# Three pieces of the second expert matrix in column halves in place of five, and twelve output rows stored in halves in place of eighteen

## The chip, the cores and the metric

One core of a Trainium2 chip runs the whole kernel. The metric is device time in microseconds (us) of one execution, as the median of several runs. A profile of one execution gives the times of every instruction and DMA packet.

## The reference

The computation is an attention stage with learned pooling, followed by a soft mixture of experts:

```python
a = softmax(phi, axis=2)                       # q, k, v: (8, 8, 576, 64); phi: (8, 8, 576, 32)
k_m, v_m = einsum(a, k), einsum(a, v)
x = softmax(q @ k_m.T / 8) @ v_m               # reshaped to x: (4608, 512)
logits = x @ moe_phi                           # (4608, 32): 8 experts with 4 slots each
d = softmax(logits, axis=0)
slot_input = d.T @ x                           # (32, 512)
slot_out[e] = relu(slot_input[e] @ w1[e]) @ w2[e]   # w1: 8 x 512 x 1024, w2: 8 x 1024 x 512
out = softmax(logits, axis=1) @ slot_out       # (4608, 512), float32
```

The change lies in the last two lines: how the second expert matrices `w2` are loaded, and in which order the output is made and stored.

## The kernel before

The kernel writes its work as a list of operations into a `Plan`. The planner gives each a time by its own cost table and sends them to the engines in that order; every engine then works through its own list in order. All transfers, loads and stores, are issued by SyncE (SP) on one queue, in the planner's order. A transfer may only be issued once the eighth transfer before it has landed, because eight semaphores take turns.

The second expert layer (`expert_out`, `mult`) reads `w2` in 16 pieces of 1 MB, two per expert. The first experts' pieces come early. The later ones come as whole matrices of 2 MB (one transfer), one single piece of 1 MB, and, for the last `NT` pieces, in column halves: `tail_out` first loads the left 256 columns of all `NT` pieces, and then the right 256 columns of all of them. A half of a piece is two transfers of 256 KB (128 partitions, two runs of 1 KB each). `tail_mult(d, n)` multiplies half `d` (0 is left, 1 is right) of tail piece `n`. The left products accumulate in the bank `kvbank`, the right products in `scbank`.

When the left products are done, `slot_sums(0)` copies the bank (L1349), sums it with a matmul (L1357) and splits the result into two parts in `sr` (L1364, L1369). From then on the left 256 columns of output rows can be made. When the right products are done, `slot_sums(1)` does the same for the right columns.

The output has 4 blocks of 128 partitions (`bp` 0 to 3) with 9 rows per partition in each (`j` 0 to 8), 36 "rows" of 128 x 512 in all, 256 KB each. A row is made on TensorE by `out_mult` (L1603: two matmuls of 256 columns for a half row, of 512 for a whole one), copied from the bank to the arena by VectorE (L1580) or ScalarE (L1579), and stored (L1616). The first two rows are made straight from the sums (`direct`, L1587).

The first `NA` groups of three rows are made in halves: their left halves while the right columns of `w2` still arrive, their right halves after the right sum. A half group is stored by one transfer of 384 KB in runs of 1 KB, except that the three rows of group 0 are stored singly (128 KB each). All later rows are made and stored whole. `RIGHT[m]` says behind which left half group the right product of tail piece `m` stands on TensorE (-1: ahead of all of them); the right sum follows the last of these.

Of the kernel before, what the change touches and what calls it, by code (L numbers as in the profile page):

```python
# [20 lines left out]
class Plan:  # L21
# [24 lines left out]
    def add(self, eng, cost, fn, r=(), w=(), also=(), pri=None, dma=0.0, slack=0.0, after=()):  # L46
        cost, ni = cost if isinstance(cost, tuple) else (cost, 4)
        i = len(self.ops)
        deps = set()
        tiles = {}  # L50
        for x in r:
            for key in x:
                tiles[key[0]] = None
                if key in self.last_w:
                    deps.add(self.last_w[key])
        for x in w:
            for key in x:
                tiles[key[0]] = None
                if key in self.last_w:
                    deps.add(self.last_w[key])  # L60
                deps.update(self.reads.get(key, ()))
        for x in w:
            for key in x:
                self.last_w[key] = i
                self.reads[key] = []
        for x in r:
            for key in x:
                self.reads.setdefault(key, []).append(i)
        deps.discard(i)
        deps.update(after)  # L70
        tiles = [t for t in tiles if t.pool is not None]
        for t in tiles:
            t.users += 1
        need = tiles + [t for t in also if t not in tiles]
        if pri is None:
            pri = self.phase[0]
            self.phase[0] += self.phase[1]
        self.ops.append((eng, cost, fn, deps, pri, dma, tiles, need, slack, ni))
        return i
# [191 lines left out]
def kernel(  # L271
# [27 lines left out]
    E, DM, FF = w1.shape  # L299
# [56 lines left out]
    def shaped(off, shape):  # L356
        n = 1
        for x in shape:
            n *= x
        a = arena[:, off: off + n]  # L360
        if len(shape) > 1:
            names = "abcd"[: len(shape)]
            a = a.rearrange(
                f"p ({' '.join(names)}) -> p {' '.join(names)}",
                **dict(zip(names[:-1], shape[:-1])),
            )
        return a, (off, n)

    def area(off, shape, n, below=(), fifo=False):

        size = shaped(off, shape)[1][1]
        xs = [shaped(off + i * size, shape) for i in range(n)]
        return Slots([a for a, _ in xs], [r for _, r in xs], below, fifo)
# [917 lines left out]
    w2s = area(W0, [2 * W_SZ], NW // 2, [ws, *early])  # L1291
    ots = area(W0, [OT_SZ], NOUT, [w2s])
    b0 = W0 + NOUT * OT_SZ
    big = {6: area(b0, [6 * DM], 1, [w2s]), 9: area(b0 + 6 * DM, [9 * DM], 1, [w2s])}
    wqs = Slots(
        [qtile[:, i * W_SZ: i * W_SZ + W_SZ] for i in range(2)],
        [(TOP + i * W_SZ, W_SZ) for i in range(2)], [qs],
# [25 lines left out]


    EG = 4
    NT, NA = 5, 6
    ONES = 2
    RIGHT = (-1, 1, 1, 2, 2)
    SLOT_AT = (20.06, 20.08, 20.1)
    hTb = hTs.tile().split(E // EG)  # L1330
    hT = lambda: hTb.ap.rearrange("p (x y) -> p x y", x=8)
# [13 lines left out]
    def slot_sums(d, middle=lambda: None):  # L1345
        x = slice(d * HD, d * HD + HD)
        add(
            *((ACT, act(HD)) if d else (DVE, dve(HD))),
            lambda: (nc.scalar.copy if d else nc.vector.tensor_copy)(  # L1349
                accs.ap[:, x], pacc[d].ap[:, 0, :HD]  # L1350
            ),
            r=[pacc[d]], w=[accs.part(d)],
        )
        y = middle()
        z = add(
            PE, 0.5,
            lambda: nc.tensor.matmul(  # L1357
                so[d].ap[:, :HD], rep.rearrange("p a n -> p (a n)"), accs.ap[:, x],
                start=True, stop=True,
            ),  # L1360
            r=[accs.part(d), rep_b], w=[so[d]], after=[y] if y is not None else (),
        )
        add(
            ACT, act(HD), lambda: nc.scalar.copy(sr.ap[:, 0, x], so[d].ap[:, :HD]),  # L1364
            r=[so[d]], w=[sr.part(d)],
        )
        add(
            DVE, dve(HD),
            lambda: nc.vector.tensor_tensor(  # L1369
                sr.ap[:, 1, x], so[d].ap[:, :HD], sr.ap[:, 0, x].bitcast(F32), op=ALU.subtract  # L1370
            ),
            r=[so[d], sr.part(d)], w=[sr.part(d)],
        )
        return z
# [109 lines left out]
    def tail_mult(d, n, after=()):  # L1484
        e, h, t = tails[n]
        return add(
            PE, (0.45, 16), lambda: mult(pacc[d].ap[:, 0], e, h, t, d),
            r=[hTb.part(e // EG), *(t.part(4 * h + 2 * d + i) for i in range(2))],
            w=[pacc[d]], after=after,
        )  # L1490
# [87 lines left out]
    def evict(dst, po, n, x):  # L1578
        return (ACT, act(n), lambda: nc.scalar.copy(dst(), po.ap[:, :n])) if x else (  # L1579
            DVE, dve(n), lambda: nc.vector.tensor_copy(dst(), po.ap[:, :n])  # L1580
        )
# [18 lines left out]
    def out_mult(bp, j, po, x):  # L1600
        y = HALF * (j % 2)
        for t in range(2):
            nc.tensor.matmul(  # L1603
                po.ap[:, : x.stop - x.start],
                cT[bp].ap[y: y + HALF, j // 2 * P: j // 2 * P + P],
                sr.ap[y: y + HALF, t, x],
                start=(t == 0),
                stop=(t == 1),
                tile_position=(y, 0),
            )  # L1610

    def store(bp, j0, x, ot, r, i=None, g=G):
        n, k = (g, 0) if i is None else (1, i)
        add(
            SP, 0.06,
            lambda: nc.sync.dma_start(  # L1616
                outv[bp * P: bp * P + P, j0: j0 + n, x],
                ot.ap.rearrange("p (g d) -> p g d", g=g)[:, k: k + n, x],
            ),
            r=r, dma=P * n * (x.stop - x.start) * 4 / (DMA_RATE if x.stop - x.start == DM else HALF_RATE),  # L1620
        )

    def half_group(d, n, single=False):
        (bp, j0), ot, x = groups[n], half[n], slice(d * HD, d * HD + HD)
        for i in range(ND if single else 0, G):
            po = b_o.tile()
            z = add(
                PE, 0.22, lambda po=po, j=j0 + i: out_mult(bp, j, po, x),
                r=[sr.part(d), cT[bp]], w=[po], also=[ot],
            )  # L1630
            y = i * DM + d * HD
            add(
                *evict(lambda y=y: ot.ap[:, y: y + HD], po, HD, (j0 + i) % 2),
                r=[po], w=[ot.part(G * d + i)],
            )
            if single:
                store(bp, j0 + i, x, ot, [ot.part(G * d + i)], i)
        if not single:
            store(bp, j0, x, ot, [ot.part(G * d + i) for i in range(G)])
        return z  # L1640
# [5 lines left out]
    for n in range(-1, NA):  # L1646
        if n >= 0:
            z = half_group(0, n, n == 0)
        for m in range(NT):
            if RIGHT[m] == n:  # L1650
                tail_mult(1, m, [z])
        if RIGHT[NT - 1] == n:
            y = slot_sums(1)
            for i in range(ND):
                y = direct(1, i, [y])
    for n in range(NA):
        half_group(1, n, n == 0)
    for bp, j0, n in ((2, 0, 3), (2, 3, 6), (3, 0, 9)):
        ot = (ots if n == G else big[n]).tile().split(n)
        for i in range(n):  # L1660
            po = b_o.tile()
            add(
                PE, 0.43,
                lambda po=po, bp=bp, j=j0 + i: out_mult(bp, j, po, slice(0, DM)),
                r=[sr, cT[bp]], w=[po], also=[ot],
            )
            add(
                *evict(lambda ot=ot, i=i: ot.ap[:, i * DM: i * DM + DM], po, DM, (j0 + i) % 2),
                r=[po], w=[ot.part(i)],
            )  # L1670
        store(bp, j0, slice(0, DM), ot, [ot], None, n)
# [31 lines left out]
```

## Time and profile before

| what | value |
|---|---|
| median of 3 runs | 200.88 us (200.79 to 200.95) |
| the profiled execution | 200.49 us |
| its span, from first to last instruction | 198.7 us |
| granted TensorE clock, mean | 0.967 of 2.4 GHz |
| TensorE busy | 168.9 us (85%) |
| VectorE busy | 141.5 us (71%) |
| ScalarE busy | 74.4 us (37%) |
| GpSimd busy | 95.5 us (48%) |
| bytes moved, mean rate | 76.47 MB, 385 GB/s |

The span is what the profiler saw of the program; the execution's own time is 1.8 us longer. Times below are from the start of the span. The 16 DMA engines are counted as one resource: a DMA share of 1 means that all 16 were busy (the shares of short stretches reach a little over 1, since packets overlap).

### The profile page before, as it was taken

The numbers are of one execution on the slowest core, as the hardware profiler recorded it, in microseconds if no ns is written. First come the engines' busy times: TensorE is split into PE (matmuls) and PEld (weight loads), VectorE is DVE, ScalarE is ACT, GpSimd is POOL, SyncE is SP. The second block draws the span as 40 slices with busy tenths as digits, with TensorE's granted clock in tenths as the row PEclk, the third lists the DMA queues.
The fourth block names the chain that finished last, engine by engine and source line by source line (L and its number), as shares of the span: only waits on it lengthen the run. The fifth ranks groups of instructions, "written<-read, shape, count | busy, mean of one in ns | idle before, by whom it ended". The sixth has DMA issues, their size and how long they took to land.

```text
span 198.7 us, 6096 instructions
## 1 busy us (share of the span) xinstructions
PE 168.9 (85%) x2607; PEld 107.7 (54%) x2607; DVE 141.5 (71%) x267; ACT 74.4 (37%) x191; POOL 95.5 (48%) x92
## 2 busy tenths in 40 slices
PE   7999747978799899888999888799999998999900
PEld 6677534645457477554666457465555543567500
DVE  7821630699898899999899998368999900558810
ACT  2022314536351665525644243120138510356600
POOL 7199303589993894979964276200005970000000
PEclk9999997999969999999999999999999999999985
DMA  6999999999999999999999999999999999999996
GB/s 198 366 392 393 384 383 390 380 391 378 404 381 386 390 381 407 381 387 402 420 422 411 417 422 421 417 422 434 422 422 422 371 315 322 360 339 343 404 418 297
DMA packets 31642, 76.47 MB, mean 385 GB/s; under 512 B 2048, under 2 KB 15872, under 8 KB 28288
## 3 DMA queue, kind: packets, MB, share of 16 engines
q1 hardware_dynamic: 31616, 76.09, 100.8%
q8 instruction: 20, 0.33, 0.7%
q14 instruction: 6, 0.05, 0.1%
HBM read 66.65 MB, written 9.44 MB: 383 GB/s over the span
## 4 chain that ended last, share of the span: by engine, by line
PE 37%; DMA 20%; DVE 14%; POOL 12%; issue 4%; SPq 4%; ACT 3%; DVEq 0%; POOLq 0%
DMA arena<-in_moe_w_dram 12%; DMA arena<-in_v_dram 9%; PE bank L1603 6%; PE scbank L813 6%; PE kvbank L704 5%; PE bank L882 4%; SPq L502 4%; POOL arena L848 3%; PE bank L1385 3%; POOL arena L871 3%; POOL arena L669 3%; POOL arena L648 3%; PE bank L1010 2%; DVE arena L606 2%; DVE arena L827 2%
## 5 line engine op out<-in xcount | busy, mean ns | idle before, releaser
L648 POOL TENSOR_TENSOR arena<-arena 128x1152 f32<-128x1152 f32 x8 | 21.0, 2632 | 17.5 <-ACT arena L641 14.9
L591 DVE STREAM_TRANSPOSE arena<-top 128x1152 f32<-128x1152 f32 x16 | 21.6, 1354 | 8.2 <-DMA top<-in_q_dram 8.2
L704 PE MATMUL kvbank<-arena 64*32 64x128 f32 x1152 | 20.9, 277 | 6.2 <-issue 2.4
L813 PE MATMUL scbank<-arena 64*64 64x288 f32 x256 | 23.6, 445 | 2.3 <-DVE arena L827 2.3
L520 PE MATMUL kvbank<-ones 128*128 128x256 f32 x82 | 23.3, 421 | 2.4 <-ACT arena L728 1.3
L669 POOL TENSOR_TENSOR arena<-arena 128x128 f32<-128x128 f32 (+2 forms) x32 | 23.3, 730 | 3.2 <-ACT arena L657 1.3
L1541 POOL TENSOR_TENSOR cT<-cS,cT 32x640 fp32r<-32x640 f32 (+1 forms) x8 | 11.3, 1414 | 26.2 <-ACT cT L1536 25.7
L871 POOL TENSOR_TENSOR arena<-arena,ssm 128x576 f32<-128x576 f32 x16 | 18.3, 1152 | 9.5 <-DVE ssm L867 7.9
L704 PEld LDWEIGHTS kvbank<-arena 64*32 64x32 f32 x1152 | 16.5, 107 | 10.8 <-issue 5.4
L848 POOL TENSOR_TENSOR arena<-arena,smx 128x576 f32<-128x576 f32 x16 | 18.4, 1152 | 7.6 <-DVE smx L843 7.6
L606 DVE TENSOR_REDUCE arena<-arena 128x128 f32<-128x1152 f32 x8 | 17.2, 2160 | 4.2 <-DMA arena<-in_phi_dram 4.1
L882 PE MATMUL bank<-arena 128*128 128x288 f32 x64 | 18.7, 425 | 1.0 <-DVE arena L874 0.8
L520 PEld LDWEIGHTS kvbank<-ones 128*128 128x128 f32 x82 | 15.7, 206 | 5.9 <-ACT arena L728 1.7
L1580 DVE COPY arena<-bank 128x256 f32<-128x256 f32 (+1 forms) x30 | 14.4, 510 | 4.9 <-PE bank L1603 3.7
L827 DVE STREAM_TRANSPOSE arena<-scbank 128x576 f32<-128x576 f32 x16 | 12.2, 764 | 5.6 <-PE scbank L813 5.5
L813 PEld LDWEIGHTS scbank<-arena 64*64 64x64 f32 x256 | 10.0, 141 | 10.1 <-DVE arena L827 3.7
L1603 PE MATMUL bank<-sr,cT 64*128 64x256 f32 (+1 forms) x100 | 15.1, 358 | 0.5 <-ACT arena L1579 0.2
L853 ACT ACTIVATE arena<-arena 128x576 f32<-128x576 f32 x16 | 10.9, 684 | 10.9 <-POOL arena L848 10.7
L882 PEld LDWEIGHTS bank<-arena 128*128 128x128 f32 x64 | 11.2, 189 | 6.2 <-DVE arena L874 2.2
L1603 PEld LDWEIGHTS bank<-sr,cT 64*128 64x128 f32 x100 | 9.9, 184 | 6.5 <-DVE arena L1580 4.1
L1579 ACT COPY arena<-bank 128x256 f32<-128x256 f32 (+1 forms) x24 | 10.4, 444 | 8.3 <-PE bank L1603 7.3
L1385 PE MATMUL bank<-arena,SIM 128*32 128x256 f32 x224 | 13.3, 392 | 0.2 <-DVE SIM L1264 0.2
(135 smaller groups left out, 263.6 us busy)
## 6 DMA issues: line engine op xcount, KB each, us to landing
arena<-in_moe_w_dram SPq DMA_DIRECT2D x19, 1024.0 KB, 14.0
top<-in_q_dram SPq DMA_DIRECT2D x8, 1152.0 KB, 12.6
arena<-in_k_dram SPq DMA_DIRECT2D x8, 1152.0 KB, 10.3
arena<-in_v_dram SPq DMA_DIRECT2D x8, 1152.0 KB, 12.7
arena<-in_moe_w_dram SPq DMA_DIRECT2D x3, 2048.0 KB, 14.3
arena<-in_moe_w_dram SPq DMA_DIRECT2D x20, 256.0 KB, 5.7
arena<-in_phi_dram SPq DMA_DIRECT2D x8, 576.0 KB, 7.2
out_dram<-arena SPq DMA_DIRECT2D x10, 384.0 KB, 4.3
```

Source lines behind the costliest of these rows:

```text
L520: lambda: nc.tensor.matmul(warm.ap, ones, ones.unsqueeze(1).to_broadcast([P, 2, P]), start=True, stop=True,),
L591: lambda: nc.vector.transpose(qT.ap.rearrange("p (i u y) -> p u i y", i=2, y=Y), qt.ap[:, h * QT_SZ: h * QT_SZ + QT_SZ].rearrange("p (u i ...
L606: lambda: nc.vector.tensor_reduce(mx.ap[:, c0:c1], ph().rearrange("p c j m -> p c m j"), axis=AX.X, op=ALU.max),
L648: lambda: nc.gpsimd.tensor_tensor(ph(), ph(), mb.ap[:, c0:c1].unsqueeze(2).to_broadcast([P, c1 - c0, J, M]), op=ALU.subtract,),
L669: plus = lambda o, x, y: nc.gpsimd.tensor_tensor(o, x, y, op=ALU.add)
L704: nc.tensor.matmul(acc.ap[M * c: M * c + M, a, : 2 * D], ph()[h0: h0 + HALF, c, j, :], kv()[h0: h0 + HALF, :, c, j * D: j * D + D], start= ...
L813: nc.tensor.matmul(scb.ap[HALF * g: HALF * g + HALF, a, :JY], pair[g].kd.ap[h0: h0 + HALF, i, c].rearrange("p r m -> p (r m)"), pair[g].qT ...
L848: lambda: nc.gpsimd.tensor_tensor(exv(), exv(), bc(mx), op=ALU.subtract),
L871: lambda: nc.gpsimd.tensor_tensor(exv(), exv(), bc(sm), op=ALU.mult),
L882: nc.tensor.matmul(lp.ap[:, :JY], vpb.ap[:, h, :], aT.ap[:, a * JY: (a + 1) * JY], start=(h == 0), stop=(h == H - 1),)
L1385: nc.tensor.matmul(hb.ap[NS * j: NS * j + NS, :256], SIM.ap[:, 2 * i + c, NS * e: NS * e + NS], wv[:, c].rearrange("p (x j t) -> p x j t", ...
L1603: nc.tensor.matmul(po.ap[:, : x.stop - x.start], cT[bp].ap[y: y + HALF, j // 2 * P: j // 2 * P + P], sr.ap[y: y + HALF, t, x], start=(t == 0),
```

## The change

`NT` goes from 5 to 3, so that two more pieces of `w2` are loaded whole; `NA` goes from 6 to 4, so that 12 rows are made and stored in halves; `RIGHT` puts the second and third right products behind group 1 (rows 3 to 5), with the first ahead of all groups as before. The six rows that were stored in halves become two stores of three whole rows, and the nine rows of block 2 are one store where they were two. A second buffer of nine rows is made in the arena.

```diff
-    big = {6: area(b0, [6 * DM], 1, [w2s]), 9: area(b0 + 6 * DM, [9 * DM], 1, [w2s])}
+    big = {6: area(b0, [6 * DM], 1, [w2s]), 9: area(b0 + 6 * DM, [9 * DM], 2, [w2s])}
...
-    NT, NA = 5, 6
+    NT, NA = 3, 4
     ONES = 2
-    RIGHT = (-1, 1, 1, 2, 2)
+    RIGHT = (-1, 1, 1)
...
-    for bp, j0, n in ((2, 0, 3), (2, 3, 6), (3, 0, 9)):
+    for bp, j0, n in ((1, 3, 3), (1, 6, 3), (2, 0, 9), (3, 0, 9)):
         ot = (ots if n == G else big[n]).tile().split(n)
```

On SP's queue, at the end of the program, the difference is this (L502 are loads, `128x4096` a whole matrix of 2 MB, `128x2x256` a transfer of 256 KB in the column layout; L1616 are stores):

```order
 L502 DMA arena<-in_moe_w_dram 128x2048 x8
-L502 DMA arena<-in_moe_w_dram 128x4096 x3
+L502 DMA arena<-in_moe_w_dram 128x4096 x4
 L502 DMA arena<-in_moe_w_dram 128x2048
-L502 DMA arena<-in_moe_w_dram 128x2x256 x20
+L502 DMA arena<-in_moe_w_dram 128x2x256 x12
```

Eight transfers of 256 KB have become one of 2 MB, which stands ahead of all column halves. The stores behind them stand in this order in the changed kernel (`128x256` is one half row, `128x3x256` a half group, `128x1536` three whole rows, `128x4608` nine):

```order
 L1616 DMA out_dram<-arena 128x256 x3
+L1616 DMA out_dram<-arena 128x3x256 x2
+L1616 DMA out_dram<-arena 128x256 x2
+L1616 DMA out_dram<-arena 128x3x256
+L1616 DMA out_dram<-arena 128x256
+L1616 DMA out_dram<-arena 128x3x256 x3
+L1616 DMA out_dram<-arena 128x1536 x2
+L1616 DMA out_dram<-arena 128x4608 x2
```

Before, all 18 left half rows stood ahead of the first right one (three single stores and five groups, then three single ones and five groups). Now only nine left half rows do; the last left group stands behind the first two right rows.

On TensorE, between the second right product of before and the right sum (`kvbank<-cS,rep`), this is gone:

```order
 L1603 MATMUL bank_62<-sr,cT 128x256 x2
-L1603 MATMUL bank_63<-sr,cT 128x256 x2
-L1431 MATMUL scbank<-arena 32x256 x4
-L1603 MATMUL bank_65<-sr,cT 128x256 x2
-L1603 MATMUL bank_62<-sr,cT 128x256 x2
-L1603 MATMUL bank_64<-sr,cT 128x256 x2
-L1603 MATMUL bank_63<-sr,cT 128x256 x2
-L1431 MATMUL scbank<-arena 32x256 x4
-L1603 MATMUL bank_65<-sr,cT 128x256 x2
-L1603 MATMUL bank_62<-sr,cT 128x256 x2
 L1357 MATMUL kvbank<-cS,rep 128x256
```

So the right sum now follows four rows behind the third right product, where a fourth and a fifth product and seven more half rows stood in between.

## Rows read from the trace of the kernel before

**Rows 1.** Busy time by stretch: engines, granted clock, DMA share, GB/s.

```profile
142.00:157.00 15.00, 15.00 (x258) 8.46 (x254) 14.17 (x45) 7.84 (x18) 5.76 (x5) 1.00 0.99 412
160.00:174.00 14.00, 12.84 (x134) 5.74 (x126) 3.43 (x9) 2.04 (x6) 2.71 (x2) 1.00 1.01 333
174.00:187.00 13.00, 12.68 (x94) 8.49 (x86) 9.71 (x22) 7.68 (x18) 0.00 (x0) 1.00 1.02 349
187.00:197.00 10.00, 2.13 (x11) 1.00 (x10) 2.44 (x4) 1.76 (x3) 0.00 (x0) 0.77 1.03 436
```

**Rows 2.** Line L502, the last left load, then the last right one: start, landing.

```profile
L502 SPq DMA_DIRECT2D arena<-in_moe_w_dram x1: 368/368/368, 161.2 to 161.2; - x1
...
DMA to landing us min/median/max: 5.5/5.5/5.5
...
L502 SPq DMA_DIRECT2D arena<-in_moe_w_dram x1: 367/367/367, 168.2 to 168.2; - x1
...
DMA to landing us min/median/max: 5.7/5.7/5.7
```

**Rows 3.** Line L1616: last left group, last right group, six rows, last nine rows.

```profile
L1616 SPq DMA_DIRECT2D out_dram<-arena x1: 372/372/372, 176.6 to 176.6; - x1
...
DMA to landing us min/median/max: 4.2/4.2/4.2
...
L1616 SPq DMA_DIRECT2D out_dram<-arena x1: 1034/1034/1034, 182.5 to 182.5; - x1
...
DMA to landing us min/median/max: 4.4/4.4/4.4
...
L1616 SPq DMA_DIRECT2D out_dram<-arena x1: 344/344/344, 186.3 to 186.3; - x1
...
DMA to landing us min/median/max: 6.1/6.1/6.1
...
L1616 SPq DMA_DIRECT2D out_dram<-arena x1: 333/333/333, 189.9 to 189.9; - x1
...
DMA to landing us min/median/max: 8.0/8.0/8.0
```

**Rows 4.** TensorE in order of time, 161 to 190 us: start, duration, instructions.

```profile
161.74 5.70 PE L1431 MATMUL kvbank<-arena 128*32 128x256 f32 x40
167.98 0.70 PE L1357 MATMUL bank<-cS,rep 128*128 128x256 f32 x2 [0.54 <-DVE cS L1349]
...
171.71 0.64 PE L1431 MATMUL scbank<-arena 128*32 128x256 f32 x8
172.28 0.74 PE L1603 MATMUL bank<-sr,cT 64*128 64x256 f32 x8
...
176.05 0.70 PE L1357 MATMUL kvbank<-cS,rep 128*128 128x256 f32 x2
...
177.54 7.06 PE L1603 MATMUL bank<-sr,cT 64*128 64x256 f32 x48
184.79 4.34 PE L1603 MATMUL bank<-sr,cT 64*128 64x512 f32 x20 [0.19 <-DVE arena L1580]
```

**Rows 5.** Issues on SP: all stores from the first on, then the first right one.

```profile
169.54 20.71 SPq L1616 DMA_DIRECT2D out_dram<-arena  x19
...
L1616 SPq DMA_DIRECT2D out_dram<-arena x1: 345/345/345, 178.0 to 178.0; - x1
```

**Rows 6.** A load issued into a part-empty queue on SP, and the busy time around it.

```profile
159.96 0.37 SPq L502 DMA_DIRECT2D arena<-in_moe_w_dram  x1
...
160.50:161.00 0.50, 0.50 (x16) 0.33 (x12) 0.00 (x0) 0.00 (x0) 0.50 (x1) 1.00 0.69 242
161.00:161.50 0.50, 0.50 (x16) 0.27 (x10) 0.00 (x0) 0.00 (x0) 0.44 (x1) 1.00 1.00 326
```

**Rows 7.** An idle time of TensorE, in order of time, and the clock behind it.

```profile
55.02 0.66 PE L748 MATMUL bank<-ident,arena 128*128 128x128 f32 x4 [1.45 <-ACT arena L721]
...
55.90:59.30 3.40, 3.40 (x48) 1.77 (x54) 3.40 (x5) 1.82 (x3) 3.40 (x4) 0.50 1.06 379
```

## The prediction

> **What bounds the kernel now.** I read the DMA share of the closing stretches first, then where the last transfers land, then TensorE's order between them. The reader should see in [rows 1] that the DMA engines are full from 142 us to 197 us, and that only the rate differs: 412 GB/s while whole matrices load, 333 and 349 GB/s while column halves are loaded and half rows are stored, 436 GB/s while whole rows are stored. Then [rows 3]: the last store is issued at 189.9 us and lands 8.0 us later, at 197.9 us, although TensorE ended at 184.79 + 4.34 = 189.13 us [rows 4]. The store before it lands at 186.3 + 6.1 = 192.4 us, so the last one had to queue. The end is therefore set by bytes and by how well the queue is fed, and TensorE has a reserve. The column halves exist to feed it: between the end of the right loads, 168.2 + 5.7 = 173.9 us [rows 2], and the first right store (issued at 178.0 us [rows 5]) the queue lives on left half rows.
>
> Unit prices. A transfer of 256 KB in column layout: the last left one lands at 161.2 + 5.5 = 166.7 us, the last right one, ten later, at 173.9 us [rows 2], so 0.72 us each. A whole matrix of 2.10 MB at 412 GB/s [rows 1]: 5.1 us. A half row: from the landing at 176.6 + 4.2 = 180.8 us to 182.5 + 4.4 = 186.9 us are 18 half rows [rows 3], so 0.34 us each. A whole row: from 192.4 to 197.9 us are nine [rows 3], so 0.61 us each.
>
> **What the change takes out.** Eight column transfers become one whole matrix: 8 x 0.72 = 5.8 us become 5.1 us, so -0.7 us. (The bounds: nothing gained, if the matrix takes 5.8 us; -1.0 us, if it moves at the 436 GB/s of [rows 1].) Six rows stored whole: 12 x 0.34 = 4.1 us become 6 x 0.61 = 3.7 us, so -0.4 us. If the queue stayed full, that would be all: **-1.1 us**.
>
> **What it moves.** The matrix now stands ahead of the left halves, which are six instead of ten. The last left half lands at 166.7 - 4 x 0.72 + 5.1 = 168.9 us, **2.2 us later**. The last right half lands at 173.9 - 0.7 = 173.2 us. The time between them, in which left rows can be made under the cover of loads, shrinks from 7.2 to 4.3 us. Two right products now come ahead of the left sum, with their whole pieces. They cost nothing: TensorE spent 5.70 us on the five left tail products from 161.74 us on [rows 4], at most 0.57 us each (171.71 to 172.28 [rows 4]), so 2.8 us of that stretch was waiting for loads. Without that cover they would cost 1.1 us.
>
> From the left sum to the third right product TensorE's order is the same, so these steps shift by 2.2 us: the left sum from 167.98 to 170.2 us, the first left store from 169.54 to 171.7 us [rows 4, 5], and the third right product from 171.71 to 173.9 us. The last right half has landed by then (173.2 us), so that wait is hidden, by 0.7 us. Behind the product (0.57 us) stand only four half rows (0.74 us, as the same four took from 172.28 us), and then the right sum: 173.9 + 1.3 = 175.2 us, where it was 176.05 us [rows 4]. ScalarE's copy of the bank fits beside those four rows. The right sum is 0.8 us earlier, though the left one is 2.2 us later.
>
> **What then waits: the queue.** The first right store follows the right sum by 178.0 - 176.05 = 1.95 us [rows 4, 5], so it is issued at 177.2 us. How soon does a store reach the engines? The trace has no store into an empty queue. The nearest is the load issued at 159.96 us, with the share at 0.69 until 161.0 us and 1.00 after it [rows 6]: **1.0 us**. The lower bound is nothing; the upper one is the 4.2 us that the last left group took from issue to landing behind a queue [rows 3], most of it queueing. I take 1.0 us. The Trainium skill (DMA: Bandwidth & Descriptors, section on latency and other measured facts) gives about 0.6 us to the first byte of such a transfer; no run here shows a lone store, and by that figure the sum below would be 0.4 us smaller, an estimate.
>
> So between 173.2 us and 177.2 + 1.0 = 178.2 us the engines have 5.0 us to fill, and SP offers nine left half rows, 9 x 0.34 = 3.1 us, since the last left group stands behind the right rows. About 1.9 us are idle, in pauses between those stores and behind them. Before, 18 half rows (6.1 us) covered 173.9 to 179.0 us: no idle time was needed.
>
> **The end, two ways.** By bytes: the last left group is the third store after the first right one, issued about 178.2 us and moving from 179.2 us. From there three left and ten right half rows (13 x 0.34 = 4.4 us) and 24 whole rows (24 x 0.61 = 14.6 us) give 198.2 us; the last bytes need some 0.5 us to be told as landed (the shares of [rows 1] end with 197.0 us and the last landing is at 197.9 us, so 0.9 at most and nothing at least; I take the middle): 198.7 us. By TensorE: rows restart 1.49 us behind the right sum (177.54 - 176.05 [rows 4]), at 176.7 us. Whole rows cost 0.40 us each (nine between the issues at 186.3 and 189.9 us [rows 3]), and the 16 half rows therefore (189.13 - 177.54 - 18 x 0.40)/16 = 0.27 us. Eleven half rows and 15 whole ones end at 176.7 + 3.0 + 6.0 = 185.7 us; the nine-row store of block 2 waits for its last row, and goes out 0.8 us later (189.13 to 189.9), at 186.5 us. It moves from 187.5 us; 18 rows are 11.0 us, and 0.5 us for the landing: 199.0 us. Before, block 2 went out in three and six rows and this limit did not exist.
>
> The later of the two counts: **199.0 us against 197.9 us, +1.1 us**. In terms: -1.1 us of transfer time, about +1.9 us idle ahead of the right rows, +0.3 us at the first right rows and the left group behind them. The profiled execution would take 200.49 + 1.1 = 201.6 us. The timed runs' median lies 0.4 us above the profiled one, so on their scale it is 200.88 + 1.1 = **202.0 us**.
>
> **Rivals.**
>
> *The queue doesn't run dry (faster).* If the first left stores reach the engines as the right loads end, and the lag between engines fills the pauses, only the transfer gain is left: 200.88 - 1.1 = 199.8 us. For it speaks that the first store is issued at 171.7 us, 1.5 us ahead of the loads' end; against it that nine half rows are 3.1 us and the hole 5.0 us, whatever their start. It decides only if the right rows come 1.9 us sooner than I have them, and the nine-row store 2 us sooner as well. The Trainium skill (DMA: Bandwidth & Descriptors, section on why small descriptors are slow) counts three more cycles for each packet: by it alone 1 KB packets lose about 8% and the change would gain, an estimate, 0.8 us. The rates of [rows 1] agree in direction (333 and 349 against 412 and 436 GB/s). Chance 0.12.
>
> *The two cancel (the same).* Starts after 0.5 us and whole rows at 0.37 us on TensorE would take 0.5 us off each and 0.45 us off the nine-row limit: 199.0 - 0.95 = 198.05 us, +0.15 us, so 201.0 us. Chance 0.18.
>
> *TensorE's clock falls (slower still).* The fourth matrix lands about 168.9 - 6 x 0.72 - 2.55 = 162.0 us (six left halves and a piece of 1 MB behind it), and TensorE is done with the third at 161.74 - 2 x 0.57 = 160.6 us: a new idle time of 1.4 us. After one of 1.45 us the granted clock was 0.50 (1.2 GHz) for 3.4 us [rows 7], from 0.9 us behind the restart. Here that would fall on 163 to 166.5 us, where TensorE waits anyway; if it comes later and meets the chain from the left sum on, it costs up to 1.7 us: 203.7 us at most, 202.9 us at the middle. Chance 0.12.
>
> **From this to the numbers.** The forecast has 0.58. Its own range is 201.3 to 202.8 us (matrix 4.8 to 5.8 us, stores reaching the engines 0.6 to 1.1 us after their issue). The range for 8 in 10 takes in the case of no change and half of the clock's: 200.7 to 203.2 us. A measurement of this kernel can tell about 0.2% (0.4 us) from no change. Faster by more: 0.12; within: 0.18; slower: 0.70.
>
> **What would show it.** In the profile after: last left load landing near 168.9 us and last right near 173.2 us; a fourth matrix, then column halves still at 0.7 us; DMA share clearly under 1 in 174 to 179 us (about 2 us of idle in sum) where it was 1.02; the right sum at about 175.2 us; the first nine-row store issued at about 186.5 us, and the two together taking 11 us. I am wrong if the share stays at 1 there, if the right sum waits for the loads, or if the first nine-row store finds a queue still long.

## The result and the profile after

The changed kernel takes 202.81 us (median of 6 runs, 202.50 to 203.73) beside 200.97 us for the kernel before in the same comparison: a ratio of 1.0099, with a 95% interval of 1.0082 to 1.0117, so about 2.0 us slower. Its profiled execution took 202.52 us with a span of 200.7 us, 2.0 us more than before in either measure. The forecast was 202.0 us.

The busy time by stretch, in the stretches of [rows 1] (columns: PE, PE load, VectorE, ScalarE, GpSimd, granted clock, DMA share, GB/s):

```profile
142.00:157.00 15.00, 15.00 (x259) 8.74 (x252) 14.10 (x46) 7.35 (x19) 5.32 (x4) 1.00 1.01 427
160.00:174.00 14.00, 11.45 (x135) 5.02 (x127) 2.03 (x5) 1.69 (x5) 3.15 (x3) 1.00 0.86 297
174.00:187.00 13.00, 13.00 (x83) 9.25 (x84) 10.05 (x21) 7.75 (x17) 0.00 (x0) 1.00 0.88 308
187.00:197.00 10.00, 2.52 (x12) 1.10 (x10) 2.81 (x5) 1.95 (x4) 0.00 (x0) 0.81 1.02 431
```

The first and the last stretch are as full as before. The two between them are not: 0.86 and 0.88 where [rows 1] had 1.01 and 1.02. The granted clock is 1.00 in the first three.

Closer, around the end of the loads and the first stores, first the kernel before and then the changed one:

```profile
171.00:173.00 2.00, 2.00 (x26) 0.99 (x18) 0.89 (x4) 0.45 (x2) 0.00 (x0) 1.00 1.10 365
173.00:177.00 4.00, 3.72 (x36) 2.32 (x35) 2.23 (x6) 2.08 (x7) 0.00 (x0) 1.00 0.99 339
177.00:180.00 3.00, 3.00 (x23) 2.08 (x21) 2.40 (x7) 1.65 (x5) 0.00 (x0) 1.00 1.03 355
```

```profile
171.00:173.00 2.00, 2.00 (x20) 1.18 (x20) 0.85 (x2) 0.74 (x2) 0.00 (x0) 1.00 0.22 77
173.00:177.00 4.00, 4.00 (x39) 2.35 (x36) 2.27 (x6) 2.05 (x6) 0.00 (x0) 1.00 0.64 210
177.00:180.00 3.00, 3.00 (x24) 2.66 (x24) 2.59 (x8) 1.57 (x5) 0.00 (x0) 1.00 0.82 270
180.00:184.00 4.00, 4.00 (x22) 2.81 (x23) 3.38 (x6) 2.80 (x6) 0.00 (x0) 1.00 1.01 341
```

There is the hole, a stretch in which the queue runs partly empty. It begins at about 171 us, and its emptiest part is 171 to 173 us, where the share is 0.22. From 180 us on the queue is full again. Counted against a share of 1, the engines idle 2 x 0.78 = 1.6 us, 4 x 0.36 = 1.4 us and 3 x 0.18 = 0.5 us, 3.5 us in all. Finer still, the DMA share of the changed kernel from 171 to 173.5 us in 40 slices of 62 ns, in tenths:

```profile
DMA  4442222312112121212121101111111369999744
```

It falls in steps, from 0.4 to 0.1, which is six and then two of 16 engines at work, and rises to full at 173.0 us, when the first stores arrive. The times of the single packets say the same: six packets are under way at 171.05 us, four at 171.3 us, and two at 172.5 and at 172.8 us.

What the DMA engines had to do as a whole, from the page's line on the queue (packets, MB, share of the span), before and after:

```profile
span 198.7 us, 6096 instructions
...
q1 hardware_dynamic: 31616, 76.09, 100.8%
```

```profile
span 200.7 us, 6051 instructions
...
q1 hardware_dynamic: 28128, 76.09, 98.7%
```

The bytes are the same, in 3488 packets fewer. Before, the packets took 1.008 x 198.7 = 200.3 us of 16 engines; after, 0.987 x 200.7 = 198.1 us: **2.2 us less** transfer time. Since the span grew by 2.0 us, 4.2 us of idle time were added. (Only the differences of these figures are used.)

Now the landings that answer to [rows 2], the last left load and then the last right one:

```profile
L502 SPq DMA_DIRECT2D arena<-in_moe_w_dram x1: 1065/1065/1065, 161.3 to 161.3; - x1
...
DMA to landing us min/median/max: 8.0/8.0/8.0
...
L502 SPq DMA_DIRECT2D arena<-in_moe_w_dram x1: 368/368/368, 167.9 to 167.9; - x1
...
DMA to landing us min/median/max: 5.5/5.5/5.5
```

They land at 169.3 and 173.4 us, within 0.4 us of the forecast. TensorE, as in [rows 4]:

```profile
162.60 0.64 PE L1431 MATMUL kvbank<-arena 128*32 128x256 f32 x8 [1.02 <-DMA arena<-in_moe_w_dram]
...
165.24 0.64 PE L1431 MATMUL kvbank<-arena 128*32 128x256 f32 x8 [0.70 <-DMA arena<-in_moe_w_dram]
...
170.55 0.70 PE L1357 MATMUL bank<-cS,rep 128*128 128x256 f32 x2 [0.54 <-DVE cS L1349]
...
174.28 0.64 PE L1431 MATMUL scbank<-arena 128*32 128x256 f32 x8
174.85 0.75 PE L1603 MATMUL bank<-sr,cT 64*128 64x256 f32 x8
175.53 0.70 PE L1357 MATMUL kvbank<-cS,rep 128*128 128x256 f32 x2
...
177.02 12.50 PE L1603 MATMUL bank<-sr,cT 64*128 64x256 f32 x70
```

TensorE waits for loads at 162.6 and 165.2 us only. The left sum (170.55 us) and the right one (175.53 us) stand within 0.4 us of the forecast, and from 177.02 us TensorE makes rows without a pause. In the hole TensorE doesn't wait for the queue; the queue waits for TensorE's rows, which begin with a left sum that stands 2.6 us later than before (167.98 us in [rows 4]).

Stores, line L1616, as in [rows 3, 5]: the first left one, the first right one, and the two of nine rows:

```profile
L1616 SPq DMA_DIRECT2D out_dram<-arena x1: 360/360/360, 172.1 to 172.1; - x1
...
DMA to landing us min/median/max: 1.8/1.8/1.8
...
L1616 SPq DMA_DIRECT2D out_dram<-arena x1: 344/344/344, 177.5 to 177.5; - x1
...
DMA to landing us min/median/max: 1.9/1.9/1.9
...
L1616 SPq DMA_DIRECT2D out_dram<-arena x1: 332/332/332, 186.7 to 186.7; - x1
...
DMA to landing us min/median/max: 7.6/7.6/7.6
...
L1616 SPq DMA_DIRECT2D out_dram<-arena x1: 332/332/332, 190.3 to 190.3; - x1
...
DMA to landing us min/median/max: 9.4/9.4/9.4
```

The first left store finds a nearly empty queue: it lands 1.8 us after its issue, where the last left group before took 4.2 us [rows 3]. The last store, issued at 190.3 us, lands 9.4 us later, behind a full queue. The end is still set by bytes; the time was lost before 180 us.

### The profile page after: what moved, and what is told of

Read it like the earlier page. It is cut to its first block, busy times and chain, and to the rows that moved or that the text cites. A ratio compares the mean times of both kernels' runs of the same rounds, so it can differ in the third digit from the quotient of the medians.

```text
span 200.7 us, 6051 instructions
## 1 busy us (share of the span) xinstructions
PE 168.2 (84%) x2595; PEld 107.9 (54%) x2595; DVE 140.7 (70%) x264; ACT 74.1 (37%) x188; POOL 95.5 (48%) x92
## 4 chain that ended last, share of the span: by engine, by line
PE 45%; DVE 14%; DMA 13%; POOL 9%; SPq 8%; issue 4%; ACT 2%; POOLq 0%; DVEq 0%
DMA arena<-in_v_dram 9%; SPq L502 8%; PE bank L1385 8%; PE bank L1603 7%; PE scbank L813 6%; PE kvbank L704 5%; PE bank L882 5%; DMA arena<-in_moe_w_dram 4%; POOL arena L871 3%; POOL arena L848 3%; PE bank L1010 2%; DVE arena L606 2%; DVE arena L591 2%; DVE smx L843 2%; DVE arena L827 2%
## 5 line engine op out<-in xcount | busy, mean ns | idle before, releaser
L1580 DVE COPY arena<-bank 128x256 f32<-128x256 f32 (+1 forms) x27 | 13.7, 547 | 3.6 <-PE bank L1603 3.4
L1603 PE MATMUL bank<-sr,cT 64*128 64x512 f32 (+1 forms) x88 | 14.5, 379 | 0.0
L1431 PE MATMUL kvbank<-arena 128*32 128x256 f32 x128 | 11.7, 383 | 2.0 <-DMA arena<-in_moe_w_dram 1.7
L874 DVE STREAM_TRANSPOSE arena<-arena 128x576 f32<-128x576 f32 x16 | 11.9, 754 | 1.5 <-POOL arena L871 1.5
```

The costliest lines, as they stand in the source:

```text
L1603: nc.tensor.matmul(po.ap[:, : x.stop - x.start], cT[bp].ap[y: y + HALF, j // 2 * P: j // 2 * P + P], sr.ap[y: y + HALF, t, x], start=(t == 0),
```

## The experiments

Two theories stood against each other from the start. **Hole**: the queue runs empty between the loads and the right rows, and the end moves by that idle time less the saved transfer time. **TensorE** (the second of the prediction's two counts): the nine-row store of block 2 goes out too late, since it waits for its last row. Differences are given against the kernel before, the ratio less 1 times 200.9 us.

**The load half of the change alone.** Three tail pieces, stores as before:

```diff
-    NT, NA = 5, 6
+    NT, NA = 3, 6
     ONES = 2
-    RIGHT = (-1, 1, 1, 2, 2)
+    RIGHT = (-1, 1, 1)
```

> Only the load half of the change: three pieces in column halves (NT = 3, right products 2 and 3 behind group 1), but 18 rows in halves and the stores of blocks 2 and 3 as before. Theory 'hole' (the queue runs dry between the end of the right loads and the first right stores, because the matrix now stands ahead of the left halves and only nine left half rows reach the queue in time): all of the loss comes with this half, +1.8 to +2.6 us against before, the DMA share well under 1 between 171 and 179 us. Rival 'rows' (the loss comes from having only 12 rows in halves): this half alone keeps the transfer gain of the loads, -0.7 us, and no more than 0.5 us of it is lost.

Measured: 203.24 us, ratio 1.011 (1.0087 to 1.0134), +2.2 us, in the range of the hole theory.

**The store half alone.** The changed kernel with five tail pieces:

```diff
-    NT, NA = 3, 4
+    NT, NA = 5, 4
     ONES = 2
-    RIGHT = (-1, 1, 1)
+    RIGHT = (-1, 1, 1, 2, 2)
```

> Only the store half of the change: 12 rows in halves (NA = 4), block 1's last six rows as two stores of three, block 2 as one store of nine; five pieces in column halves as before. Theory 'hole': 12 left half rows (4.1 us of transfers) stand against some 5 us from the end of the right loads to the first right store, so about 0.8 us of idle against 0.4 us gained by whole rows: 0 to +0.8 us against before. Rival 'rows': +1.5 us or more.

Measured: 201.84 us, ratio 1.0047 (1.0031 to 1.0062), +0.9 us: a little over the hole theory's 0.8 us, and short of the rival's 1.5 us. The windows of the load half with its line on the queue, then the windows of the store half:

```profile
171.00:173.00 2.00, 2.00 (x20) 1.08 (x19) 0.97 (x3) 0.82 (x3) 0.00 (x0) 1.00 0.35 121
173.00:177.00 4.00, 4.00 (x38) 2.46 (x36) 2.43 (x7) 2.12 (x7) 0.00 (x0) 1.00 0.64 213
177.00:180.00 3.00, 2.92 (x26) 1.99 (x25) 2.50 (x7) 1.86 (x6) 0.00 (x0) 1.00 0.82 272
...
q1 hardware_dynamic: 29584, 76.09, 98.8%
```

```profile
171.00:174.00 3.00, 3.00 (x40) 1.54 (x34) 1.51 (x4) 0.65 (x2) 0.00 (x0) 1.00 1.10 357
174.00:177.00 3.00, 2.29 (x26) 1.34 (x25) 1.18 (x3) 1.02 (x3) 0.00 (x0) 1.00 0.96 330
177.00:180.00 3.00, 3.00 (x21) 2.13 (x20) 1.99 (x5) 1.80 (x5) 0.00 (x0) 1.00 0.54 185
```

Each half makes a hole. With fewer column halves the queue is nearly empty from 171 us, until left rows flow, and has pauses up to 180 us: that is nearly the whole hole of the change. With fewer half rows it is full until 177 us and half empty behind it (0.54), since the left rows run out before the right ones come.

The load half keeps 18 half rows, and they don't help it. The planner has put SP's stores in another order there: in its trace only nine left half rows go out ahead of the first right one, as in the whole change, where it was 18 before (and is 12 in the store half alone). So the two costs do not add (2.2 + 0.9 against 2.0 together). The saved transfer time does divide: the load half has 0.988 x 201.4 = 199.0 us of transfers, 1.3 us under before (1.5 us if the packets' times are summed, without the rounding of the share), which leaves 0.7 to 0.9 us of the 2.2 us for the stores. (The profiled execution of the store half took 202.78 us, 0.9 us over its median, so its own line is not used.)

**The nine-row store split.** The changed kernel with block 2 in three and six rows:

```diff
-    for bp, j0, n in ((1, 3, 3), (1, 6, 3), (2, 0, 9), (3, 0, 9)):
+    for bp, j0, n in ((1, 3, 3), (1, 6, 3), (2, 0, 3), (2, 3, 6), (3, 0, 9)):
```

> The changed kernel with block 2 stored as three and six rows, as before, in place of nine at once. Theory 'hole': no difference to the changed kernel beyond 0.3 us (+1.6 to +2.2 us against before), since the nine-row store was issued at 186.70 us while the queue still had work until 188.8 us. Rival 'nine rows' (the limit that the prediction counted as the later one: the store waits for TensorE's 15th whole row): 0.5 to 1.0 us faster than the changed kernel.

Measured: 203.06 us, ratio 1.0096 (1.007 to 1.0122), +1.9 us: as the whole change. The TensorE theory falls. This is the store of three rows ahead of the nine-row one in the changed kernel:

```profile
L1616 SPq DMA_DIRECT2D out_dram<-arena x1: 740/740/740, 183.1 to 183.1; - x1
...
DMA to landing us min/median/max: 5.7/5.7/5.7
```

It landed at 188.8 us, 2.1 us behind the nine-row issue at 186.7 us, so the queue never waited for that issue.

**The last right product further back.** The third one stands behind all four left groups:

```diff
-    RIGHT = (-1, 1, 1)
+    RIGHT = (-1, 1, 3)
```

> The changed kernel with the third right product, and so the right sum, behind all four left groups (RIGHT = (-1, 1, 3)), so that 12 left half rows stand ahead of the first right one in place of nine. Theory 'hole': 1.0 us of transfers moves into the hole, while the right rows start 0.6 to 0.9 us later: 0 to 0.5 us faster than the changed kernel. Rival 'late right sum' (the end counts from the first right row, and a later right sum only costs): 0.6 to 0.9 us slower than the changed kernel.

Measured: 202.74 us, ratio 1.0091 (1.0064 to 1.0117), +1.8 us; not to be told from the changed kernel. Twelve left half rows now go out ahead of the first right one in place of nine, and that one goes out at 178.7 us in place of 177.5 us: what the first gives the second takes, as I read it.

**How many column halves.** The kernel before with four pieces (`RIGHT = (-1, 1, 1, 2)`) and with six (`(-1, 1, 1, 2, 2, 3)`), and the changed kernel with one (`(-1,)`):

```diff
-    NT, NA = 5, 6
+    NT, NA = 4, 6
...
-    NT, NA = 5, 6
+    NT, NA = 6, 6
...
-    NT, NA = 3, 4
+    NT, NA = 1, 4
```

> Four pieces in column halves in place of before's five (right products at -1, 1, 1, 2), 18 rows in halves and all stores as before: half of the load part. Theory 'hole': 15 left half rows (5.8 us at 0.385 us each) still stand ahead of the first right one against some 5 us, so the queue runs nearly dry only for a short while, and 0.6 us of transfer time is saved: -0.3 to +0.6 us against before. Rival 'each piece costs' (the loss grows with each piece that goes ahead of the left halves, +2.2 us for two of them): +1.1 us.

> Before with six pieces in column halves in place of five: the opposite of the load part of the change. Theory 'hole': one more piece moves in 1 KB packets, 0.6 to 0.7 us more of transfer time, and there is only some 0.2 us of idle left to cover: +0.3 to +0.8 us against before. Rival 'an earlier left sum always helps': 0.5 us or more faster than before.

> One step further than the change: one piece in column halves (NT = 1), 12 rows in halves. Transfer time falls by another 1.2 us, the left sum moves back by another 2 us, and the right loads end 1.2 us earlier. Theory 'hole': the idle time grows by more than the transfer time falls, 2.2 to 3.2 us slower than before (0.3 to 1.2 us slower than the changed kernel). Rival 'bytes' (the end follows the transfer time once the hole is there): 0.5 to 1.2 us faster than the changed kernel.

Measured: four pieces 202.04 us, ratio 1.0051 (1.0032 to 1.007), +1.0 us. The hole theory missed this, and the rival's +1.1 us was met. In 171 to 174 us the share is already 0.77 there, so the hole begins sooner than the theory had it. Six pieces 201.02 us, ratio 1.0009 (0.9993 to 1.0025), not to be told from before, where the theory had 0.3 to 0.8 us more: by the packets' times 0.7 us of transfer time was added, and why so little of it shows at the end is open. One piece 203.98 us, ratio 1.0147 (1.0121 to 1.0173), +3.0 us, in the theory's range. Fewer halves are worse in each step, and more than five bring nothing. The single piece shows the hole at its largest:

```profile
160.00:171.00 11.00, 6.63 (x92) 3.05 (x84) 0.00 (x0) 0.00 (x0) 2.73 (x2) 0.84 0.86 341
171.00:174.00 3.00, 2.44 (x33) 1.51 (x22) 0.42 (x1) 0.37 (x1) 0.00 (x0) 1.00 0.07 23
174.00:177.00 3.00, 3.00 (x25) 1.78 (x23) 1.86 (x5) 1.77 (x5) 0.00 (x0) 1.00 0.36 116
177.00:180.00 3.00, 2.97 (x23) 2.27 (x22) 2.65 (x8) 1.44 (x5) 0.00 (x0) 1.00 0.67 217
```

A part of it may be TensorE's clock. TensorE waited 3.00 us for a whole matrix that landed at 167.4 us, and behind that wait its granted clock was 0.5 (1.2 GHz) for 3.4 us; this is the 0.84 of the first line. Eight matmuls took 1.08 us there and 0.61 us ahead of it. So the prediction's rival of the falling clock, which didn't happen in the changed kernel, happens here. Its price is 0.6 us at most, an estimate: the last left half landed at 171.17 us, a product takes 0.57 us, and the last left one ended at 172.32 us.

**How many half rows.** The kernel before with 21 of them:

```diff
-    NT, NA = 5, 6
+    NT, NA = 5, 7
...
-    for bp, j0, n in ((2, 0, 3), (2, 3, 6), (3, 0, 9)):
+    for bp, j0, n in ((2, 3, 3), (2, 6, 3), (3, 0, 9)):
```

> Before with 21 rows in halves in place of 18 (NA = 7): a step the other way. Theory 'hole': the queue of before is already full there (DMA share 1.03 from 171 to 180 us), so three more rows in halves only cost transfer time, 6 x 0.385 - 3 x 0.61 = 0.5 us: +0.2 to +0.6 us against before. Rival 'rows' (more left rows always help): 0.2 us or more faster than before.

Measured: 201.54 us, ratio 1.0032 (1.002 to 1.0044), +0.6 us. The queue was full (a share of 1.08 in 171 to 177 us, 1.04 in 177 to 180 us), so more half rows bring their slower transfer, with nothing to cover (by the packets' times 0.4 of the 0.6 us). A queue that is full has no use for more cover.

**Left half rows stored singly.** The changed kernel, so that the first bytes of each left group leave earlier:

```diff
-            if single:
+            if single or d == 0:
                 store(bp, j0 + i, x, ot, [ot.part(G * d + i)], i)
-        if not single:
+        if not single and d:
```

> The changed kernel with each left half row stored singly (128 KB) in place of groups of three, same order of rows, so that a row reaches the queue as soon as it is copied. Theory 'hole': the pauses between the left stores (near 174.2, 176.5 and 178.2 us) shrink, 0.3 to 0.8 us faster than the changed kernel. Rival 'right rows decide' (the queue is empty until the right rows come, whatever the left ones do): no difference beyond 0.2 us.

Measured: 203.97 us, ratio 1.0156 (1.0132 to 1.0179), +3.1 us, 1.1 us slower than the changed kernel. Both expectations missed. The store issued at 177.2 us, and the busy time behind it in steps of half a microsecond:

```profile
L1616 SPq DMA_DIRECT2D out_dram<-arena x1: 1679/1679/1679, 177.2 to 177.2; - x1
...
177.50:178.00 0.50, 0.50 (x6) 0.31 (x4) 0.50 (x3) 0.18 (x1) 0.00 (x0) 1.00 0.73 248
178.00:178.50 0.50, 0.50 (x7) 0.47 (x6) 0.38 (x2) 0.39 (x2) 0.00 (x0) 1.00 0.08 25
178.50:179.00 0.50, 0.50 (x7) 0.50 (x5) 0.35 (x2) 0.40 (x2) 0.00 (x0) 1.00 0.08 10
```

SP issued the single stores 0.49 us apart (eight from 173.77 to 177.21 us, with waits of only 17 ns between them), and a half row is 0.385 us of transfer (131,072 bytes at the 341 GB/s of 180 to 184 us), so SP no longer keeps the queue filled. Then one issue took 1.68 us, and the queue was nearly empty (0.08) for over a microsecond. What held that issue is not shown: an instruction packet (queue q8) of 16 KB runs at about that time, but one does so in the other traces too.

**Left rows early.** If the hole is what costs, then filling its front must give the time back. In the next three kernels the left products of the tail pieces are left out, so the left sum lacks them and left rows begin before the last loads; all transfers stay. First the changed kernel, then the kernel before as a control:

```diff
-                    stop=(e == E - 1 and h == 1),
+                    stop=(e == E - 1 and h == 1) or (d == 0 and 2 * e + h == 2 * E - NT - 1),
...
-    for n in range(NT):
-        tail_mult(0, n)
```

> The changed kernel without the left products of the three tail pieces (left out, so the left columns lack these pieces); all loads and stores stay. The left sum no longer waits for the left column halves, and the left stores are in the queue before the right loads end. Theory 'hole': nearly all idle time (4.1 us) goes, and the end follows the transfer time, which is 2.2 us under before's: 1.4 to 2.3 us faster than before, 3.2 to 4.3 us faster than the changed kernel. Rival 'right rows decide' (the end counts from the right sum): less than 1 us faster than the changed kernel.

> Control: the kernel before without the left products of its five tail pieces (left out likewise). Theory 'hole': its queue is full there anyway, so leaving them out gains little, 0 to 0.6 us against before. Rival (the left-out work itself is what pays in the run beside it): over 1 us faster.

Measured: the changed kernel 201.53 us, ratio 1.003 (1.0018 to 1.0043), +0.6 us, so 1.4 us given back; the control 200.98 us, ratio 1.001 (0.9993 to 1.0027), no difference. For the changed kernel both expectations missed: the theory had 3.2 to 4.3 us given back, its rival less than 1 us. In the changed kernel the windows are now:

```profile
171.00:174.00 3.00, 2.74 (x24) 0.66 (x22) 0.16 (x1) 0.06 (x1) 0.00 (x0) 1.00 1.04 357
174.00:177.00 3.00, 2.52 (x18) 1.65 (x14) 0.90 (x3) 1.14 (x4) 0.00 (x0) 1.00 0.59 207
177.00:180.00 3.00, 3.00 (x24) 2.31 (x24) 2.25 (x7) 1.83 (x5) 0.00 (x0) 1.00 0.45 140
```

The front of the hole is filled (1.04), and its back is deeper: the twelve half rows are used up between 175.3 and 177 us, and the first right store is issued at 176.8 us. So the hole has two parts: until the left rows flow, and from where they run out until the right rows flow. The load half of the change opens both, the store half the second.

**Both parts covered.** The last run takes the loads of the change, the 18 half rows of before, and the early left rows:

```diff
-    NT, NA = 5, 6
+    NT, NA = 3, 6
     ONES = 2
-    RIGHT = (-1, 1, 1, 2, 2)
+    RIGHT = (-1, 1, 1)
...
-                    stop=(e == E - 1 and h == 1),
+                    stop=(e == E - 1 and h == 1) or (d == 0 and 2 * e + h == 2 * E - NT - 1),
...
-    for n in range(NT):
-        tail_mult(0, n)
```

> The kernel before with three pieces in column halves (RIGHT = (-1, 1, 1), six half-stored groups and stores as before), and without the left products of the three tail pieces, so that the left sum lacks them and the left rows start before the last loads. Theory of a hole in two parts (until the left rows flow, and until the right rows flow): both are now covered, the first by early left rows, the second by 18 half rows, at about 0.385 us each 6.9 us, which last from about 171 to 178 us. Then the end follows the transfer time, which in the run with three pieces and six groups was 1.5 us less than before: 199.4 us, and not over 200.4 us with some idle time left; DMA share near 1 in all of 171 to 180 us. Rival, that early left rows don't help because the queue is held by something other than the sums (the spacing of issues, or the number of transfers in flight): 201 us or more, with a share clearly under 1 in 174 to 180 us although left rows are ready.

Measured: 199.37 us, ratio 0.9924 (0.9909 to 0.9939), **1.5 us faster** than before, as expected, and 3.7 us faster than the first experiment. That one has the same transfers; what differs is the left products and, through them, SP's order: here all 18 left half rows go out ahead of the first right one, there nine. Its windows and its line on the queue:

```profile
171.00:173.00 2.00, 2.00 (x25) 1.11 (x23) 1.06 (x3) 0.66 (x2) 0.00 (x0) 1.00 1.03 355
173.00:177.00 4.00, 3.52 (x23) 2.14 (x24) 1.34 (x4) 1.61 (x5) 0.00 (x0) 1.00 1.05 360
177.00:180.00 3.00, 2.99 (x24) 2.50 (x24) 2.53 (x7) 1.92 (x6) 0.00 (x0) 1.00 0.98 332
...
q1 hardware_dynamic: 29584, 76.09, 100.7%
```

The queue is as full as before (100.7% of 197.2 us against 100.8% of 198.7 us), and the span is shorter by nearly what the transfers save: 200.3 - 198.6 = 1.7 us of transfers, 1.5 us of span. Saved transfer time does reach the end here, since the queue stays fed.

This kernel leaves out work, so it is no version to use; among the kernels that compute everything none was faster than before. An order that makes the left sum this early with all its products, such as the left halves loaded ahead of the last whole matrix, was not tried.

## Why the prediction was right in direction, and short in size

- **What bounds the kernel: right.** Bytes and the feeding of the queue set the end. The last experiment shows it: the same bytes, a fed queue, 1.5 us faster; and by the control, leaving out left products gains nothing where the queue is fed anyway.
- **What it moves: right.** The last left load was forecast at 168.9 us and landed at 169.3 us, the last right one 173.2 and 173.4 us, the right sum 175.2 and 175.53 us, the first right store 177.2 and 177.5 us, the first nine-row store 186.5 and 186.7 us. The hidden wait of the third right product held: TensorE is busy in all nine microseconds from 171 to 180 us.
- **What the change takes out: mis-sized, 1.1 us forecast and 2.2 us measured.** The step that failed is "Unit prices". They came from the distance between landings, 0.72 us for 256 KB and 0.34 us for a half row, which would be 364 and 386 GB/s. [rows 1] already said 333 and 349 GB/s. The full stretch from 180 to 184 us, which is half rows for the most part, gives 341 GB/s after, so 131,072 bytes take 0.385 us. With these prices the sum is 8 x 0.79 - 4.9 (2.10 MB at 427 GB/s) = 1.4 us for the loads and 12 x 0.385 - 6 x 0.61 = 1.0 us for the rows, together 2.4 us, near the 2.2 us measured. Term by term: 0.7 us was forecast for the loads, and the load half alone has 1.3 to 1.5 us less on the queue; 0.4 us was forecast for the rows, and 0.7 to 0.9 us is left for them.
- **What then waits: the mechanism was right, and its start was wrong.** The hole was put at 173.2 to 178.2 us, with 1.9 us idle in it and 0.3 us behind. From 173 us on the windows show 1.4 + 0.5 = 1.9 us, against 2.2 us forecast. What was missing is the 1.6 us ahead of it, from 171 to 173 us. I had taken the queue as full until the last load lands. A landing is the last piece's: four right loads (1.05 MB) still landed between 171 and 173.5 us, while the engines moved only 77 GB/s x 2 us = 0.15 MB in 171 to 173 us. The rest of those bytes had been moved before 171 us. So a few engines were late with their part (shares of 0.4 to 0.1, six to two of 16), and the others had nothing left to do. The feeding by left rows began when the left sum allowed it, as forecast; the loads stopped filling the queue 2 us sooner than forecast.
- **One error behind both terms.** Where landings follow each other faster than bytes flow, the late engines are catching up, as I read it. That makes the prices too low, and hides that the other engines run dry first.
- **The sum.** -2.2 us of transfer time; idle +1.6 us before 173 us and +1.9 us from there on; another +0.3 us since before moved 2 x 1.10 + 4 x 0.99 + 3 x 1.03 = 9.25 us of transfers in these nine, where I count nine. That is 1.6 us of the 2.0 us. By the times of the packets, 0.2 us more stands ahead of 142 us and 0.2 us behind 180 us; where these come from is not shown (each kernel has one trace). That the forecast came within 0.9 us is partly luck: 1.1 us too little saved and 2.0 us too little idle time have opposite signs.
- **The end, two ways: the choice was wrong, at 0.3 us.** "The later of the two counts" was TensorE's, and splitting that store changed nothing. The count by bytes binds. It gave 198.7 us for the end and the last store landed at 190.3 + 9.4 = 199.7 us. 13 half rows at 0.385 us in place of 0.34 us are 0.6 us of that miss. A first nine-row store that finds a long queue was one of the prediction's own signs of being wrong, and it came: the store ahead of it landed 2.1 us behind its issue.
- **A store's first bytes after 1.0 us: held.** Ahead of the packets of four stores the queue had run dry, or nearly so. They were issued at 172.12, 173.60, 175.92 and 177.52 us, and packets set in again at 172.99, 174.45, 176.83 and 178.36 us: 0.84 to 0.91 us after the start of the issue, about 0.5 us after its end. The Trainium skill (DMA: Bandwidth & Descriptors, section on latency and other measured facts) gives about 0.6 us to the first byte; it lies between these two counts. The same section gives some 2 us as the fixed cost of a transfer; here a lone store of 128 KB took 1.8 us with its bytes, somewhat less.
- **The rivals.** "The queue doesn't run dry" failed by the share of 0.22. "The two cancel" needed stores that start after 0.5 us and whole rows at 0.37 us on TensorE; they started after 0.9 us, and nine rows between the issues at 186.7 and 190.3 us are 0.40 us each. "TensorE's clock falls" did not happen: idle times of 1.02 and 0.70 us came (1.4 us was forecast), and the granted clock was 1.00 in every stretch shown up to 187 us. It did happen with one tail piece, behind 3.00 us of waiting.
- **Packets of 1 KB.** The Trainium skill (DMA: Bandwidth & Descriptors, section on why small descriptors are slow) counts about three more cycles per packet, which I estimate at some 8% for 1 KB. The rates after, 341 GB/s with half rows and 427 to 431 GB/s with whole matrices and rows, differ by 20%: the direction agrees, and that overhead alone is too small for it.

## What to carry to other kernels

Price a transfer by the bytes per second of a stretch in which the queue is full, never by the distance between landings, and date the end of a stream of loads by the fall of the DMA share, not by its last landing. When a queue must be fed between two phases, ask two things apart: when does the cover begin, and how long does it last; a change that weakens both makes two holes, and a saving in transfer time shows at the end only if neither is there.

## What was not expected of the hardware

- **Engines run dry 2 us before the last landing.** In 171 to 173 us the mean share was 0.22 while loads still landed; with the load half alone it was 0.35, with one tail piece 0.07 over 171 to 174 us. The trace doesn't say which engines are late.
- **A pause around an instruction packet.** In each of the fourteen traces one 16 KB packet of an instruction queue starts between 174.5 and 178.5 us and takes 0.9 to 1.6 us. In the kernel before, whose queue is full, it ends at 176.0 us, and the only dip between 174.3 and 178 us begins 0.5 us later (0.8, 0.6, 0.4, 0.3 and 0.6 in slices of 0.1 us from 176.5 us on). That the packet causes the dip was not tested.
- **A small store takes longer to issue than to move.** Eight stores of 128 KB in a row went out 0.49 us apart, while each takes 0.385 us to move.
